# Loading the key weights before the first filter piece, and starting TensorE on the key blocks

## The chip, the cores and the metric

The kernel runs on one core of a Trainium2 chip. The core has five engines with instruction streams of their own: TensorE (PE: matrix products, with PEld for the loading of weights), VectorE (DVE), ScalarE (ACT), GpSimd (POOL) and SyncE (SP, which here only issues transfers). Sixteen DMA engines carry the transfers. The metric is the device time of one execution in microseconds (us), and a kernel is compared by the median of its runs.

## The reference

Two independent computations on 2048 rows of 576 columns stand side by side in the output.

```python
# A: a short causal filter of k times v, then a long causal convolution along the rows
k_shift = sum over t of k_pad[:, t:t+S, :] * shift_k[:, ks-1-t]      # ks = 4 taps
kv  = k_shift * v
y   = irfft(rfft(pad(kv)) * rfft(pad(ssm_k)))[:S] + kv * ssm_D
a   = q * y
# B: linear attention, 32 heads of 18 columns
q, k, v = split(x @ wqkv);  phi = lambda t: where(t > 0, t + 1, exp(t)) + 1e-6
kv  = phi(k)^T v per head;  z = sum of phi(k)
b   = (phi(q) kv / (phi(q) z + 1e-6)) @ wo
out = concatenate([a, b], axis=-1)
```

## The kernel before

The convolution of part A is done as a two-stage Fourier transform by matrix products with constant tables. The filter `ssm_k` (`hs`, in five pieces of 128 or 96 columns) is turned by TensorE (the helper `h_piece`, L479), written from PSUM to the tiles `hT`, and multiplied in the first stage (`s1`, L510) with the table `Gsb`, which is loaded in two halves. One `s1` block is four products into a pair of PSUM banks, and ACT or DVE writes it to `Ch` (L241 for ACT, L243 for DVE). An `s1` block reads one half of `Gsb`: blocks 384, 390, 392, 382 of the first channel group the first half, blocks 378, 380, 386, 388 the second. `s2` (L560), `inv` and `inv2` (L615, L640) follow, for the filter and then for the signal.

Part B projects `x`. The first quarter of the rows comes as two pairs of row blocks (`x_pairs`): each pair is loaded (`x_sb`), its last 64 columns are copied to `x4` (L241 or L245), and TensorE turns it with the identity in `idw` (L366), eight products and two more for `x4`; the result goes to `xT` (L243 or L241). Then `kproj` (L688) makes ten products for a key block of 128 rows, ACT the exponential (L693) and DVE the rest of phi (L696). `qproj` (L710) does the same for queries, five products at a time. The other quarters of `x` are turned by transposing transfers (L388, L390).

Before data has come, TensorE works on constants: the op `fill` (L930) multiplies a tile of ones nine times, and each of `NF` ops `fil2` (L937) four times. Nothing reads the results.

The order of all work is written out by hand. `PLAN` is a list of ops, each with a letter for its engine (P TensorE, A ScalarE, D VectorE, G GpSimd, S SyncE) and the number in which it was recorded; an engine runs its ops in the order of the list. `PLACES` gives each buffer its address or PSUM bank in the same order of recording. The numbers that matter here: 844 is `fill`, 845 and 846 are `fil2`; S26 and S28 load the two pairs of `x`, S15 the identity, S54 and S53 the key weights `wk`; S369, S421, S363, S470, S476 load the filter pieces in that order, S19 and S18 the halves of `Gsb`, S56 and S55 the query weights `wq`. P30 and P32 turn the first pair of `x`, P36 and P34 the second. P92 and P89 are the first two key blocks, P95 the third. P373 and P370 turn the first filter piece, P422 and P424 the second, P366 and P364 the third, P471 the first half of the fourth.

All loads go through one queue of SyncE in list order, and SyncE has eight semaphores for them: a load waits until the load eight places before it in the list has landed. SyncE's order in the section on the change shows these waits as DMAHW and a number.

Of the kernel before, what the change touches and what calls it, by code (L numbers as in the profile page):

```python
# [29 lines left out]
EP, WX = True, False  # L30
PW, QE, NF = False, True, 2
ACC = [(0, 1), (2, 1)]
# [164 lines left out]
def kernel(  # L197
# [26 lines left out]
    P = Prog()  # L224
# [104 lines left out]
    if WX:  # L329
        load("wjb", Wr, lambda e: dma(e, Wr.t[:].rearrange("p d j -> p (d j)"), ap(A_shift_k, 0, [[0, 128], [1, 4 * D]])), 589824, 4608)  # L330
        for i in range(3):
            P.op("AD", lambda e, i=i: copy(e, Wj.t[:, :, CC * i:CC * i + CC], Wr.t[:, CC * i:CC * i + CC, :].rearrange("p d j -> p j d")),
                 rd=[Wr], wr=[(Wj, i)], name="wjx", n=4 * CC)
    else:
# [4 lines left out]
             rd=[wtok], wr=[(Wj, i) for i in range(3)])  # L339
# [414 lines left out]
    for t in range(5):  # L754
# [8 lines left out]
         wr=[(wo5, "m")])  # L763
# [7 lines left out]
    def kvmm(e):  # L771
# [8 lines left out]
        rd=[kps, cst], wr=[(kvb, 0)], name="kvev", n=504)  # L780
    P.op("D", lambda e: nc.vector.tensor_tensor(
        out=kvb.t[0:72, 4, 0:72], in0=kps.t[0:72, 1, 0:72], in1=maskbd()[0:72, 0:72], op=ALU.mult),
        rd=[kps, cst], wr=[(kvb, 1)], name="kvev", n=72)
    zps = psb(1, "zps")

    def zmm(e):
# [10 lines left out]
        rd=[zps, cst], wr=[(zsel, 1)], name="zev", n=32)  # L797
# [9 lines left out]
    for f in range(2):  # L807
# [21 lines left out]
        if PW:  # L829
# [7 lines left out]
            wr=[den], name="den+", n=256)  # L837
# [90 lines left out]
    def fmm(e):  # L928
        for j in range(9):
            nc.tensor.matmul(fps.t[:, 0, :], lhsT=cft.t[:, 0:128], rhs=cft.t[:], start=True, stop=True)  # L930
    P.op("P", fmm, rd=[cft], wr=[fps], name="fill", mm=[(512, 128, 128)] * 9)
    for i in range(NF):
# [29 lines left out]
PLAN = """  # L962
G7 D843 P844 P845 S26 S15 P30 G4 G6 A27 P846 P32 G2 G11 G12 G3 S369 P373 D31 S54 S53 G0 A375 P370 A371 A372 D33 S20
G376 S22 P92 A93 P89 D94 S28 G13 G29 P36 P34 A37 D35 S421 P422 A374 A23 S19 G5 P424 D425 A90 S363 A423 D91 P95 A96 D97
P441 A442 P433 P366 D367 P364 D365 G368 G377 G8 A434 S470 P431 P471 A432 P392 A393 D472 P390 D391 G475 P384 A385 S18
P378 D379 S56 P380 A381 S55 G426 S476 P388 P386 A387 P382 A383 P427 P435 A436 D389 D428 P439 A440 D394 D412 P429 A430
P437 A438 P137 D403 A138 D139 P98 A99 D100 S24 P417 P395 P419 A420 A418 A396 D443 P473 D461 D474 P149 S58 A150 P399
A400 P413 P401 P404 S41 D151 D452 P397 A398 P146 A147 A405 P140 A141 D142 P408 A409 A402 D148 S59 P479 A480 A414 S60
G42 G57 G1 G10 S25 D64 P143 P477 P459 A144 D145 G9 P464 A465 P462 A463 S40 A478 G481 P158 A159 D160 P161 P415 P466 D65
A460 P468 A469 A467 A416 A162 D163 P164 P152 S51 P406 P457 A458 A407 P410 A411 P444 A445 S50 G52 P191 P453 P455 D72  # L970
# [46 lines left out]
"""  # L1017
# [30 lines left out]
```

## Time and profile before

| | before |
|---|---|
| median of 3 runs | 155.97 us |
| the runs | 155.5, 155.97, 158.14 us |
| the profiled execution: device time | 156.14 us |
| its span, first to last instruction | 154.4 us |
| granted TensorE clock, mean | 0.997 |
| busy: PE / DVE / ACT / POOL | 147.8 / 136.2 / 134.6 / 63.9 us |

The profile is of one execution. The span leaves out 1.74 us of its device time, before the first and after the last instruction. The page divides the span in slices and names for each engine how busy it was; the chain of waits follows the work that ended last back to the start. Of SyncE's rows, the time shown is that of issuing a transfer and not of the transfer itself. When a transfer landed can be read where an engine waited for it.

### The profile page before, as it was taken

The page shows a single profiled execution, that of the slowest core. Times are in us where ns is not written, and L with a number is a line of the kernel's source. Part 1 is how long each engine was busy: PE and PEld are TensorE (multiplying, and loading weights), DVE is VectorE, ACT ScalarE, POOL GpSimd, SP SyncE. Part 2 cuts the span into 40 slices and gives each one's busy share as a digit, 9 for nine tenths or more (in the row PEclk, how much of TensorE's full clock was granted, in tenths as well). Part 3 has the DMA queues.
Part 4 walks back from the last instruction along what each step waited for, and adds up shares of the span by engine and source line. Part 5 has one row for each costly group of instructions (what it writes and reads, how often), then busy time and mean ns, then how long its engine had stood idle before and what let it go on. Part 6 is the DMA issues. An engine that isn't in the chain of part 4 may idle for free.

```text
span 154.4 us, 4061 instructions
## 1 busy us (share of the span) xinstructions
PE 147.8 (96%) x1609; PEld 115.9 (75%) x1609; DVE 136.2 (88%) x161; ACT 134.6 (87%) x247; POOL 63.9 (41%) x57
## 2 busy tenths in 40 slices
PE   6999999999999999999999999899999999999980
PEld 2489975664758789788888887668767899999970
DVE  1027999999999999899999999999899999999980
ACT  3068999999999979896999999999999999999760
POOL 6020406003164954611170669998590005307500
PEclk9999999999999999999999999999999999999998
DMA  5899998999891038007961797699998999955895
GB/s 138 273 397 289 278 217 363 202 178 243 318 400 42 0 67 358 0 0 132 287 252 57 231 218 211 201 280 288 387 388 327 373 377 302 204 151 143 253 310 155
DMA packets 26717, 35.84 MB, mean 232 GB/s; under 512 B 15882, under 2 KB 21003, under 8 KB 25930
## 3 DMA queue, kind: packets, MB, share of 16 engines
q1 hardware_dynamic: 25834, 32.96, 69.2%
q0 software_dynamic: 864, 2.62, 9.3%
q8 instruction: 12, 0.20, 0.5%
q14 instruction: 7, 0.06, 0.1%
HBM read 20.76 MB, written 4.99 MB: 167 GB/s over the span
## 4 chain that ended last, share of the span: by engine, by line
PE 91%; ACT 5%; DVE 1%; issue 0%
PE ps_all L710 15%; PE ps_all L899 13%; PE ps_all L739 13%; PE ps_all L688 13%; PE ps_all L615 9%; PE ps_all L510 9%; PE ps_all L640 5%; PE ps_all L560 5%; PE ps_all L479 3%; PE ps_all L930 3%; ACT Ch L241 2%; PE ps_all L937 1%; ACT sph L241 1%; DVE spu L243 1%; PE ps_all L821 1%; PE ps_all L366 1%
## 5 line engine op out<-in xcount | busy, mean ns | idle before, releaser
L710 PE MATMUL ps_all<-xT,wq 128*126 128x512 bf16 (+1 forms) x100 | 24.2, 382 | 0.0
L899 PE MATMUL ps_all<-M,pqT 126*128 126x288 bf16 (+1 forms) x160 | 22.5, 287 | 0.0
L688 PE MATMUL ps_all<-wk,xT 128*128 128x288 bf16 x160 | 20.9, 286 | 0.0
L445 DVE TENSOR_TENSOR m<-kh,Wj 128x6144 bf16<-128x6144 bf16 x6 | 20.1, 3348 | 0.0
L688 PEld LDWEIGHTS <-xT 128*128 128x128 bf16 x160 | 17.4, 110 | 2.9
L899 PEld LDWEIGHTS <-pqT 126*128 126x128 bf16 (+1 forms) x160 | 16.6, 110 | 3.2 <-issue 1.4
L710 PEld LDWEIGHTS <-wq 128*126 128x126 bf16 (+1 forms) x100 | 12.4, 132 | 7.7 <-issue 1.5
L260 POOL TENSOR_TENSOR m<-m 128x1536 bf16<-128x1536 bf16 x4 | 12.4, 3095 | 13.7 <-DVE pqT L257 6.3
L241 ACT ACTIVATE Cu<-ps_all 128x768 bf16<-128x768 f32 x22 | 17.6, 859 | 0.2 <-PE ps_all L510 0.2
L510 PEld LDWEIGHTS <-Gsb 128*128 128x128 bf16 x192 | 16.2, 98 | 2.0 <-issue 1.0
L739 PE MATMUL ps_all<-pk,x_sb 128*128 128x289 bf16 (+1 forms) x128 | 17.1, 287 | 0.0
L241 ACT ACTIVATE Ch<-ps_all 128x768 bf16<-128x768 f32 x20 | 15.7, 846 | 1.4 <-PE ps_all L510 1.4
L260 POOL TENSOR_TENSOR pqT<-pqT,rb 126x1024 bf16<-126x1024 bf16 (+1 forms) x7 | 15.3, 2195 | 3.6 <-DMA X<-sph 2.4
L241 ACT ACTIVATE sph<-ps_all 128x512 bf16<-128x512 f32 x31 | 16.6, 618 | 0.0
L241 ACT ACTIVATE V<-ps_all 128x512 bf16<-128x512 f32 x30 | 16.3, 645 | 0.1
L615 PE MATMUL ps_all<-Esb,sph 128*128 128x128 bf16 x144 | 15.7, 219 | 0.0
L696 DVE SCALAR_TENSOR_TENSOR pk<-ek,ps_all 128x576 bf16<-128x576 bf16 x16 | 11.8, 751 | 3.9 <-ACT ek L693 3.8
L241 ACT ACTIVATE spu<-ps_all 128x512 bf16<-128x512 f32 x27 | 14.6, 616 | 0.2 <-PE ps_all L560 0.2
L739 PEld LDWEIGHTS <-x_sb 128*128 128x128 bf16 x128 | 12.4, 98 | 2.9
L713 ACT ACTIVATE eq<-ps_all,neg 126x512 bf16<-126x512 f32 (+1 forms) x20 | 13.4, 705 | 1.0 <-PE ps_all L710 1.0
L615 PE MATMUL ps_all<-Esb,X 128*128 128x128 bf16 x112 | 13.7, 219 | 0.0
L615 PEld LDWEIGHTS <-sph 128*128 128x128 bf16 x144 | 12.9, 98 | 0.5 <-issue 0.4
(95 smaller groups left out, 304.1 us busy)
## 6 DMA issues: line engine op xcount, KB each, us to landing
X<-sph SPq DMA_DIRECT2D x18, 256.0 KB
v<-in_A_v_dram SPq DMA_DIRECT2D x2, 1152.0 KB
out_dram<-ob SPq DMA_DIRECT2D x16, 144.0 KB
q<-in_A_q_dram SPq DMA_DIRECT2D x1, 2304.0 KB
out_dram<-q SPq DMA_DIRECT2D x11, 192.0 KB
rb<-r_scr SPq DMA_DIRECT2D x8, 252.0 KB
x_sb<-in_B_x_dram SPq DMA_DIRECT2D x3, 576.0 KB
kh<-in_A_k_dram SPq DMA_DIRECT2D x1, 1584.0 KB
```

Of the source, the lines that this page charges most:

```text
L241: nc.scalar.activation(out=o, in_=i, func=ACTF.Copy)
L260: return (nc.vector if e == "DVE" else nc.gpsimd).tensor_tensor(out=o, in0=a, in1=b, op=op)
L445: return nc.vector.tensor_tensor(out=m.t[:], in0=i0, in1=i1, op=ALU.mult)
L510: nc.tensor.matmul(ps.t[:, bank, lo - 384 * bank:hi - 384 * bank], lhsT=Gsb.t[:, b, ri, :], rhs=src[:, lo - CC * j:hi - CC * j], start=Tru ...
L560: nc.tensor.matmul(ps.t[32 * j:32 * j + 32, kh - k0, :], lhsT=W2()[32 * kh:32 * kh + 32, :], rhs=ct.t[32 * kh:32 * kh + 32, 8 * j:8 * j + ...
L615: nc.tensor.matmul(ps.t[:, hh, 128 * c:128 * c + 128], lhsT=src.t[:, 4 * (h0 + hh) + c, :], rhs=Esb.t[:, 32 + wi, :], start=(wi < 2), stop ...
L688: nc.tensor.matmul(ps.t[:, hh, 0:HALF], lhsT=cols(xT.t[0:KT[t], t, :], r), rhs=wk.t[0:KT[t], t, HALF * hh:HALF * hh + HALF], start=(t == 0 ...
L696: P.op("D", lambda e: nc.vector.scalar_tensor_tensor(out=pk[r // 4].t[:, r % 4, 0:D].rearrange("p (h c) -> p h c", h=2), in0=eb.t[:], scal ...
L710: nc.tensor.matmul(ps.t[0:hn, c - c0, :], lhsT=wq.t[0:KT[t], t, HCH[c][0]:HCH[c][0] + hn], rhs=xT.t[0:KT[t], t, :], start=(t == 0), stop=( ...
L713: P.op("A", lambda e: nc.scalar.activation(out=eb.t[0:hn], in_=ps.t[0:hn], func=ACTF.Exp, bias=neg1.t[0:hn, :]), rd=[ps, neg1], wr=[eb], n ...
L739: nc.tensor.matmul(ps.t[0:m, 0, 0:n], lhsT=x4[r // 4].t[:, r % 4, :] if t == 4 else x_sb[r // 4].t[:, r % 4, 128 * t:128 * t + 128], rhs=p ...
L899: nc.tensor.matmul(ps.t[:, hh - h, 0:HALF], lhsT=cols(pqT[r // 8].t[0:128 if c == 4 and not EP else hn, c, 512 * (r // 4 % 2):512 * (r // ...
```

## The change

Four edits, nearly all in the list of the order.

- `fill` has five products in place of nine, and there is one `fil2` in place of two. The one that is left stands behind both turns of the first pair of `x`.
- The loads of the key weights (S54, S53) stand ahead of the load of the first filter piece (S369), behind the identity.
- The first two key blocks (P92, P89, with their work on ACT and DVE) stand ahead of the turns of the first filter piece (P373, P370). One of the three writes of that piece to `hT`, op 372, goes from ACT to DVE.
- The `s1` blocks 378 and 382 change places, their writes to `Ch` with them: the write at the earlier place stays on DVE and the one at the later place on ACT.

```diff
-PW, QE, NF = False, True, 2
+PW, QE, NF = False, True, 1
...
     def fmm(e):
-        for j in range(9):
+        for j in range(5):
             nc.tensor.matmul(fps.t[:, 0, :], lhsT=cft.t[:, 0:128], rhs=cft.t[:], start=True, stop=True)
...
-G7 D843 P844 P845 S26 S15 P30 G4 G6 A27 P846 P32 G2 G11 G12 G3 S369 P373 D31 S54 S53 G0 A375 P370 A371 A372 D33 S20
+G7 D843 P844 S26 S15 S54 S53 P30 G4 G6 A27 P32 P845 G2 G11 G12 G3 D31 D33 G0 S369 S20 S22 S28 P92 A93 P89 D94 A90 D91
...
-P378 D379 S56 P380 A381 S55 G426 S476 P388 P386 A387 P382 A383 P427 P435 A436 D389 D428 P439 A440 D394 D412 P429 A430
+D383 S56 P380 A381 S55 G426 S476 P388 P386 A387 P378 A379 P427 P435 A436 D389 D428 P439 A440 D394 D412 P429 A430 P437
```

SyncE at the program's start, before, with the waits on earlier loads (`hs` are the filter pieces; DMAHW0 is the semaphore of the first and the ninth load, DMAHW1 that of the second and the tenth, and so on):

```order
L234 DMA x_sb_3_74<-in_B_x_dram 128x1152
L234 DMA idw_76<-tab_i 128x288
L234 DMA hs_104<-in_A_ssm_k_dram 128x2048
L234 DMA wk_97<-in_B_wqkv_dram 64x576
L234 DMA wk_97<-in_B_wqkv_dram 128x4x576
L234 DMA Drow_134<-in_A_ssm_D_dram 1x576
L234 DMA srow_137<-in_A_shift_k_dram 64x36
L234 DMA x_sb_3_74<-in_B_x_dram 128x1152
L234 DMA hs_178<-in_A_ssm_k_dram 128x2048 [waits DMAHW0_49]
L234 DMA Gsb_191<-tab_g 128x2048 [waits DMAHW1_49]
L234 DMA hs_205<-in_A_ssm_k_dram 128x2048 [waits DMAHW2_49]
L234 DMA hs_255<-in_A_ssm_k_dram 96x2048 [waits DMAHW3_49]
```

And now:

```order
L234 DMA x_sb_3_66<-in_B_x_dram 128x1152
L234 DMA idw_68<-tab_i 128x288
L234 DMA wk_70<-in_B_wqkv_dram 64x576
L234 DMA wk_70<-in_B_wqkv_dram 128x4x576
L234 DMA hs_103<-in_A_ssm_k_dram 128x2048
L234 DMA Drow_105<-in_A_ssm_D_dram 1x576
L234 DMA srow_107<-in_A_shift_k_dram 64x36
L234 DMA x_sb_3_66<-in_B_x_dram 128x1152
L234 DMA hs_173<-in_A_ssm_k_dram 128x2048 [waits DMAHW0_49]
L234 DMA Gsb_186<-tab_g 128x2048 [waits DMAHW1_49]
L234 DMA hs_198<-in_A_ssm_k_dram 128x2048 [waits DMAHW2_49]
L234 DMA hs_247<-in_A_ssm_k_dram 96x2048 [waits DMAHW3_49]
```

The two key-weight loads have passed the first filter piece. From the sixth place on, the order of the loads is the same.

ScalarE's first work on data, before (`x_6` is `x4`, `ek` the exponentials of key blocks, `Ch` the writes of `s1` blocks):

```order
L241 ACTIVATE x_6_88<-x_sb_3_74 128x2x64
L241 ACTIVATE hT_13_120<-ps_all 128x8x64
L241 ACTIVATE hT_14_130<-ps_all 128x8x64
L241 ACTIVATE hT_13_120<-ps_all 128x8x64
L693 ACTIVATE ek_149<-ps_all,neg_12_118 128x576
L241 ACTIVATE xT_11_114<-ps_all 128x256
L241 ACTIVATE hT_14_130<-ps_all 128x8x64
L241 ACTIVATE srt_189<-srow_137 64x36
L693 ACTIVATE ek_203<-ps_all,neg_12_118 128x576
L241 ACTIVATE hT_13_120<-ps_all 128x8x128
L693 ACTIVATE ek_219<-ps_all,neg_12_118 128x576
L241 ACTIVATE Ch_226<-ps_all 128x4x96x2 x3
```

And now:

```order
L241 ACTIVATE x_7_83<-x_sb_3_66 128x2x64
L693 ACTIVATE ek_120<-ps_all,neg_11_101 128x576
L693 ACTIVATE ek_133<-ps_all,neg_11_101 128x576
L241 ACTIVATE hT_17_152<-ps_all 128x8x64
L241 ACTIVATE hT_19_157<-ps_all 128x8x64
L241 ACTIVATE xT_10_98<-ps_all 128x256
L241 ACTIVATE hT_19_157<-ps_all 128x8x64
L241 ACTIVATE srt_184<-srow_107 64x36
L241 ACTIVATE hT_17_152<-ps_all 128x8x128
L693 ACTIVATE ek_211<-ps_all,neg_11_101 128x576
L241 ACTIVATE Ch_218<-ps_all 128x4x96x2 x3
```

The exponentials of the first two key blocks come first, and one write to `hT` is gone from ScalarE. From the first `Ch` on, its order is the same but for the two exchanged blocks, which read alike.

More of the change, by code (lines that the diff above doesn't have):

```diff
@@ L928, in fmm @@
     def fmm(e):
-        for j in range(9):
+        for j in range(5):
             nc.tensor.matmul(fps.t[:, 0, :], lhsT=cft.t[:, 0:128], rhs=cft.t[:], start=True, stop=True)
-    P.op("P", fmm, rd=[cft], wr=[fps], name="fill", mm=[(512, 128, 128)] * 9)
+    P.op("P", fmm, rd=[cft], wr=[fps], name="fill", mm=[(512, 128, 128)] * 5)
     for i in range(NF):
@@ L962 @@
 PLAN = """
[L963 to L969 removed]
+G7 D843 P844 S26 S15 S54 S53 P30 G4 G6 A27 P32 P845 G2 G11 G12 G3 D31 D33 G0 S369 S20 S22 S28 P92 A93 P89 D94 A90 D91
+P373 P370 A375 G13 G29 A371 D372 G376 P36 P34 A37 D35 S421 P422 A374 A23 S19 G5 P424 D425 S363 A423 P95 A96 D97 P441
+A442 P433 P366 D367 P364 D365 G368 G377 G8 A434 S470 P431 P471 A432 P392 A393 D472 P390 D391 G475 P384 A385 S18 P382
+D383 S56 P380 A381 S55 G426 S476 P388 P386 A387 P378 A379 P427 P435 A436 D389 D428 P439 A440 D394 D412 P429 A430 P437
+A438 P137 D403 A138 D139 P98 A99 D100 S24 P417 P395 P419 A420 A418 A396 D443 P473 D461 D474 P149 S58 A150 P399 A400
+P413 P401 P404 S41 D151 D452 P397 A398 P146 A147 A405 P140 A141 D142 P408 A409 A402 D148 S59 P479 A480 A414 S60 G42
+G57 G1 G10 S25 D64 P143 P477 P459 A144 D145 G9 P464 A465 P462 A463 S40 A478 G481 P158 A159 D160 P161 P415 P466 D65
 A460 P468 A469 A467 A416 A162 D163 P164 P152 S51 P406 P457 A458 A407 P410 A411 P444 A445 S50 G52 P191 P453 P455 D72
```

2 rows, old and new, of the table PLACES are left out of this document.

## The prediction

> **What bounds the kernel now.** I read the page first: who is busy, and what the chain of waits is made of.
>
> ```profile
> PE 147.8 (96%) x1609; PEld 115.9 (75%) x1609; DVE 136.2 (88%) x161; ACT 134.6 (87%) x247; POOL 63.9 (41%) x57
> PE 91%; ACT 5%; DVE 1%; issue 0%
> ```
>
> TensorE is the bound by a long way. The waits of TensorE say the same: in the whole span its idle time is the start and two small gaps.
>
> ```profile
> PE ps_all L930 <- DVE cft L926: 1.5, 1, 1.5
> PE ps_all L850 <- ACT M L241: 0.3, 1, 0.3
> PE ps_all L560 <- DVE spu L243: 0.2, 1, 0.2
> ```
>
> So taking work from TensorE's front should pay in full, unless that work is only filling time in which data is on its way. The timeline of TensorE (start, length, line, count) shows the opening; L930 and L937 are the constant products, L366 the turns of `x`, L479 those of the filter, L688 key blocks, L510 `s1` blocks.
>
> ```profile
> 1.45 4.02 PE L930 MATMUL ps_all<-cft 128*128 128x512 bf16 x9 [1.45 <-DVE cft L926]
> 5.27 1.65 PE L937 MATMUL ps_all<-cft 128*128 128x512 bf16 x4
> 6.75 0.61 PE L366 MATMUL ps_all<-idw,x_sb 128*128 128x128 bf16 x8
> 7.20 1.03 PE L937 MATMUL ps_all<-cft 128*128 128x512 bf16 x4
> 8.06 0.28 PE L366 MATMUL ps_all<-idw,x 128*128 128x128 bf16 x2
> 8.17 1.16 PE L479 MATMUL ps_all<-idw,hs 128*128 128x128 bf16 x16
> 9.17 2.61 PE L688 MATMUL ps_all<-wk,xT 128*128 128x288 bf16 x20
> 11.62 0.28 PE L366 MATMUL ps_all<-idw,x 128*128 128x128 bf16 x2
> ...
> 12.18 1.16 PE L479 MATMUL ps_all<-idw,hs 128*128 128x128 bf16 x16
> ...
> 15.12 1.16 PE L479 MATMUL ps_all<-idw,hs 128*128 128x128 bf16 x16
> 16.17 0.49 PE L510 MATMUL ps_all<-hT,Gsb 128*128 128x192 bf16 x4
> 16.50 0.65 PE L479 MATMUL ps_all<-idw,hs 96*128 96x96 bf16 x8
> 16.98 5.24 PE L510 MATMUL ps_all<-hT,Gsb 128*128 128x192 bf16 x52
> ```
>
> From start to start, a constant product took (5.27 - 1.45)/9 = 0.424 us at first and (8.06 - 7.20)/4 = 0.215 us later: the clock doubles between 5.3 and 7.2 us, and the turns at 6.75 already run at (7.20 - 6.75)/8 = 0.056 us each.
>
> When the data lands is told by SyncE, which waits before issuing a load until the load eight places earlier has landed. Its timeline, its waits in the stretches 0 to 6.5, 6.4 to 8.7, 10.5 to 13 and 13 to 16.4 us, and ScalarE's first work on `x`:
>
> ```profile
> 6.45 1.11 SPq L234 DMA_DIRECT2D hs<-in_A_ssm_k_dram  x2
> 8.56 0.34 SPq L234 DMA_DIRECT2D Gsb<-tab_g  x1
> ...
> 10.08 0.51 SPq L234 DMA_DIRECT2D hs<-in_A_ssm_k_dram  x1
> 12.95 0.68 SPq L234 DMA_DIRECT2D w_scr<-srt  x1
> 16.31 0.33 SPq L234 DMA_DIRECT2D kh<-in_A_k_dram  x1
> ```
>
> ```profile
> SPq L234 <- DMA hs<-in_A_ssm_k_dram: 0.5, 1, 0.5
> SPq L234 <- DMA wk<-in_B_wqkv_dram: 1.0, 1, 1.0
> SPq L234 <- DMA hs<-in_A_ssm_k_dram: 0.4, 1, 0.4
> SPq L234 <- DMA hs<-in_A_ssm_k_dram: 1.0, 1, 1.0
> ```
>
> ```profile
> 3.64 0.31 ACT L241 ACTIVATE x<-x_sb 128x128 bf16<-128x128 bf16 x1 [1.63 <-DMA x_sb<-in_B_x_dram]
> ```
>
> Read together: the first pair of `x` landed by 3.64, the first filter piece by 6.45, the key weights by 8.56, the second filter piece at 10.08 + 0.51 + 0.4 = 11.0, the third at 12.95 + 0.68 + 1.0 = 14.6. TensorE turned that third piece at 15.12: 0.5 us behind its landing. The rest follows from the rate (busy times of stretches; the last column is GB/s, so thousands of bytes per us):
>
> ```profile
> 11.00:12.20 1.20, 1.20 (x18) 1.06 (x16) 0.76 (x1) 0.67 (x2) 0.14 (x1) 1.00 1.00 406
> 12.30:14.60 2.30, 2.30 (x30) 2.05 (x29) 1.91 (x3) 2.16 (x5) 0.00 (x0) 1.00 1.08 253
> 14.60:16.10 1.50, 1.50 (x24) 1.46 (x22) 0.85 (x3) 1.49 (x3) 0.00 (x0) 1.00 0.99 270
> 16.10:17.80 1.70, 1.70 (x25) 1.69 (x24) 1.70 (x4) 1.70 (x4) 0.38 (x1) 1.00 1.09 307
> ```
>
> The queue is full (DMA share, the column before, about 1.0) and serves loads in their order. The fourth piece, 96 x 2048 x 2 = 393 KB, needs 393/270 = 1.5 us after 14.6 and lands near 16.1; it is used at 16.50. The second half of `Gsb`, 524 KB, needs 524/307 = 1.7 us and lands near 17.8; block 378, the fourth from 16.98 at 0.33 us each, uses it near 18.0. These two are estimates. So behind a TensorE that never idles stands a transfer queue only 0.2 to 0.5 us ahead of it.
>
> **The change part by part.** *The shorter opening, by work alone.* Five products end at 1.45 + 5 x 0.424 = 3.57. The turns need the identity, queued behind `x`: 74 KB at 253 to 406 KB per us, 0.2 to 0.3 us after 3.64, say 3.9. The ten turns now run at the slow clock, 0.424/4 = 0.106 us each: 4.97. Four slow products: 6.67. The two key blocks take 11.62 - 9.17 = 2.45, to 9.12; the filter's turns 9.17 - 8.17 = 1.0, to 10.12. Before, this place is 11.62. By work alone the change is worth 1.50 us: 2.34 of constant products removed (3.82 + 1.48 + 0.86 before, 9 x 0.424 now), less 0.5 for turns at the slow clock and 0.33 of waiting.
>
> *The loads exchanged.* The key weights (664 KB) no longer wait behind 524 KB of filter. Between 6.45 and 8.56 the queue moved those 664 KB, 314 KB per us, so they land about 524/314 = 1.7 us earlier, at 6.9: 0.2 us after TensorE is ready for them, which moves 10.12 to 10.35. The first filter piece lands in their stead, by 8.56, ahead of its use at 9.35. On SyncE's queue the exchange passes nothing else; Drow, `srow` and the second pair of `x` stand behind the same sum of bytes as before. The key blocks also wait for the write of the turned `x`:
>
> ```profile
> 7.40 0.69 DVE L243 COPY xT<-ps_all 128x1024 bf16<-128x1024 bf16 x1 [6.00 <-PE ps_all L366]
> 8.37 0.29 DVE L243 COPY xT<-ps_all 128x256 bf16<-128x256 bf16 x1 [0.28 <-PE ps_all L366]
> ```
>
> Those are 0.98 us from about 4.9, done by 5.9 under the `fil2` products; without that cover they would hold the key blocks until 5.9, still ahead of the weights.
>
> *From 10.35 on, data decides.* The second pair of `x` was used at 11.62; SyncE's load at 10.08 waits for it and shows no wait, so it has landed by then. Its turns take 12.18 - 11.62 = 0.56, to 10.9. The second filter piece lands at 11.0: about 0.1 of waiting. From there to the third piece is 15.12 - 12.18 = 2.94 of work, to 14.0; the third piece lands at 14.6, so TensorE stands for 0.6 and starts at about 14.7, 0.4 ahead of now. To the fourth piece are 16.50 - 15.12 = 1.38, to 16.1, which is when it lands. I put its start at 16.2, a gain of 0.3; the ends are 0.1 (it is used now within 0.4 of its estimated landing) and 0.4.
>
> *The exchanged `s1` pair.* Block 382 needs only the first half of `Gsb`. With 378 in its place, TensorE would ask for the second half at 16.7 + 3 x 0.33 = 17.7 and wait 0.1 for 17.8; block 380, now the first to need it, comes at 18.0. The cover is worth at most 0.1. The other engine's side: the chain of waits goes over to ScalarE here.
>
> ```profile
> 17.15 0.35 PE ps_all L510 x4
> 17.49 0.02 issue
> 17.52 2.27 ACT Ch L241 x3
> ```
>
> ScalarE's write at 17.52 is released by TensorE's block at 17.15, so it moves with that block, by the same 0.3, and what follows with it. The writes exchanged between DVE and ScalarE are one for one, and op 372, moved to DVE, lies ahead of 14.6, where both wait for data: nothing.
>
> *Sum.* 1.50 by work, 1.2 of it lost to the queue: 0.3 gained, between 0 and 0.6. The profiled execution, 156.14 us (span 154.4 and 1.74 around it), becomes 155.85; it stands 0.17 above the median of the three runs. The median 155.97 becomes 155.7.
>
> **The rivals.** *The transfers come sooner* (25%). From 12.3 on the queue moves 253 to 307 KB per us, just before 406. No row names a reason, and it may not recur. At 406 the third piece lands at 12.3 + 524/406 = 13.6 and TensorE reaches it at 14.0 in place of 15.12: a gain of 1.1, to 154.9. Against it: the slow stretch holds over three different loads in a row.
>
> *The key weights land no sooner* (9%), if their rows of 1152 bytes are slow wherever they stand. At 8.56 the key blocks would end at 11.0 and the filter's turns at 12.05, 0.4 behind now; the third piece would be reached at 15.5, behind its landing, and 0.4 us stay: 156.4, slower. This decides from a landing later than about 8.1. For it: nothing else can run on TensorE in that wait, since the filter's turns now stand behind. Against it: the 314 KB per us above is no slower than the rows of the filter.
>
> *The clock comes later* (8%). [...]
>
> **How the numbers follow.** Forecast 58%, 155.7, its own range 155.2 to 156.1 (gain 0 to 0.6 and the spread of the runs, 155.5 to 156.1 without the one at 158.14). A range of 154.5 to 156.6 takes in the faster transfers and the milder slow cases. Two per cent, 3.1 us, is about what a measurement of this kernel can tell from no change; even the whole opening block, 6.2 us of which 2.3 go, is not enough for that: faster 2%. Slower by so much takes the late clock and more: 3%. Within: 95%.
>
> **What the changed kernel's profile would show.** TensorE starts the turns at 3.9 and the key blocks at 6.7 to 6.9. It now shows waits for `hs` at L479, about 0.6 us ahead of the third piece (near 14.0) and little ahead of the second and fourth; the constant work turned into idle time. The third piece starts near 14.7, the fourth near 16.2, ScalarE's `Ch` writes run on from 17.2, and after 22 us every row is as before, 0.3 us earlier. I am wrong if TensorE has no wait at the third piece (then the queue was sooner and the gain nears 1.1), if the key products start after 8 us, or if they take 0.245 us each beyond 10 us.

## The result and the profile after

The changed kernel took 158.57 us, median of four runs (158.21 to 159.26); the kernel before took 156.88 in the same comparison (four runs, 155.5 to 158.14). The ratio is 1.0147, with a 95% interval of 1.0107 to 1.0187: slower by about 1.5%, which is inside 2%, but outside the range of the prediction and on its other side. Three more measurements of the same kernel, told below, gave 1.0051, 1.0056 and 1.0061. The size of the loss differs, its sign does not. Ratios leave out executions more than 1.5% longer than the fastest of the same kernel and so need not equal the quotient of the medians, which are over all executions.

The profiled execution of the changed kernel took 159.26 us, its span 157.5. Its page, with the lines on the engines, on the granted clock over the span in 40 slices (9 is full) and on the chain of waits:

```profile
PE 149.2 (95%) x1601; PEld 116.4 (74%) x1601; DVE 137.2 (87%) x162; ACT 134.6 (85%) x246; POOL 64.0 (41%) x57
...
PEclk9999999999999999999999999956999999999998
...
PE 72%; DMA 13%; DVE 5%; ACT 4%; SPq 3%; issue 1%; DVEq 0%
```

The clock row before:

```profile
PEclk9999999999999999999999999999999999999998
```

TensorE issues eight matmuls less and is busy 1.4 us longer. The clock row shows why: near 102 us the granted clock falls. And the chain, which was 91% TensorE, now leads through transfers for 13% of the span. The opening itself came out as wished. TensorE's timeline:

```profile
3.78 1.01 PE L366 MATMUL ps_all<-idw,x_sb 128*128 128x128 bf16 x8
...
4.80 1.83 PE L937 MATMUL ps_all<-cft 128*128 128x512 bf16 x4
6.71 2.61 PE L688 MATMUL ps_all<-wk,xT 128*128 128x288 bf16 x20
...
11.58 1.17 PE L479 MATMUL ps_all<-idw,hs 128*128 128x128 bf16 x16 [0.71 <-DVE hT L243]
...
14.47 1.18 PE L479 MATMUL ps_all<-idw,hs 128*128 128x128 bf16 x16
...
15.88 0.65 PE L479 MATMUL ps_all<-idw,hs 96*128 96x96 bf16 x8
```

The third filter piece starts at 14.47 in place of 15.12, the fourth at 15.88 in place of 16.50. To see where that went, the start of the same matmul in both traces is enough. The table gives changed kernel minus kernel before, in us, at places named by the time before; two later profiles, of the kernel before and of the changed kernel, stand beside it.

| place (us before; line) | kernel before, again | changed | changed, third time |
|---|---|---|---|
| 12.18 L479 | -0.11 | -0.60 | -0.68 |
| 22.09 L710 | -0.08 | -0.54 | -0.62 |
| 81.60 L739 | +0.32 | -0.07 | -0.25 |
| 100.61 L560 | +0.63 | +1.08 | -0.25 |
| 105.37 L510 | +0.60 | +3.92 | -0.24 |
| 112.10 L899 | +2.11 | +3.92 | +0.48 |
| 114.60 L899 | +2.29 | +3.34 | +0.66 |
| span, us | 156.3 | 157.5 | 154.6 |

In the first profile of the changed kernel the gain of about half a microsecond lives until 78 us, shrinks at 80 and is lost at 99. The other two profiles in the table also lose 1.5 and 0.7 us between 105 and 112 us. The waits of TensorE in the changed kernel name the places:

```profile
PE ps_all L850 <- DMA wo<-in_B_wo_dram: 1.3, 1, 1.3
PE ps_all L479 <- DVE hT L243: 0.7, 1, 0.7
PE ps_all L510 <- DVE v L260: 0.3, 1, 0.3
```

At 80 us VectorE's products with the second half of the signal `v` come late, at 99 us the weights of the output projection, `wo`. TensorE's rows at L850, before and after:

```profile
99.73 0.94 PE L850 MATMUL ps_all<-wo,kvb 126*126 126x288 bf16 x6 [0.31 <-ACT M L241]
```

```profile
100.16 0.95 PE L850 MATMUL ps_all<-wo,kvb 126*126 126x288 bf16 x6 [1.25 <-DMA wo<-in_B_wo_dram]
```

The chain of waits goes over exactly these two transfers:

```profile
72.47 7.29 DMA v<-in_A_v_dram
...
79.85 0.96 DVE v L260
...
91.28 8.83 DMA wo<-in_B_wo_dram
...
100.16 0.47 PE ps_all L850 x2
```

Behind the second wait comes the clock. The stretches 98 to 102 and 102 to 104 us (busy times with counts; then granted clock, DMA share, GB/s):

```profile
98.00:102.00 4.00, 2.43 (x42) 1.38 (x30) 2.96 (x6) 2.97 (x6) 3.92 (x2) 1.00 0.47 160
102.00:104.00 2.00, 2.00 (x30) 1.02 (x20) 2.00 (x4) 1.91 (x5) 1.25 (x1) 0.50 0.94 304
```

TensorE is busy for 2.43 of 4 us, and then runs at half clock, by the trace's clock record from 101.98 for 6.83 us. That is the step from +1.08 to +3.92. In the same four microseconds the DMA engines were busy for 0.47 of the time (0.84 before), and between 96 and 98 us, with `wo` still on its way, for 0.28 of it (0.45 before). So the end of `wo` was not late for want of bandwidth.

So one execution tells a story: 0.5 us gained, 0.5 lost at `v`, 1.15 at `wo`, 2.8 at the clock, 0.6 made up again behind it. Of the four executions of the changed kernel only this one has the low granted clock (0.975 in the mean; 0.993 to 1.000 in the others), and the others still took 158.2 to 158.6 us. And the changed kernel's third profile, 154.6 us, has neither the wait for `wo` nor the clock's fall, and the kernel before has both 154.4 and 156.3. What belongs to the change and what to chance had to be found by runs.

### The profile page after: what moved, and what is told of

Read it like the earlier page. It is cut to its first block, busy times and chain, and to the rows that moved or that the text cites. A ratio compares the mean times of both kernels' runs of the same rounds, so it can differ in the third digit from the quotient of the medians.

```text
span 157.5 us, 4046 instructions
## 1 busy us (share of the span) xinstructions
PE 149.2 (95%) x1601; PEld 116.4 (74%) x1601; DVE 137.2 (87%) x162; ACT 134.6 (85%) x246; POOL 64.0 (41%) x57
## 4 chain that ended last, share of the span: by engine, by line
PE 72%; DMA 13%; DVE 5%; ACT 4%; SPq 3%; issue 1%; DVEq 0%
PE ps_all L710 14%; PE ps_all L899 14%; PE ps_all L688 13%; PE ps_all L615 9%; DMA wo<-in_B_wo_dram 6%; PE ps_all L640 5%; PE ps_all L560 5%; DMA v<-in_A_v_dram 5%; PE ps_all L510 4%; PE ps_all L739 4%; SPq L234 3%; PE ps_all L479 3%; DMA wk<-in_B_wqkv_dram 3%; DVE m L445 2%; ACT Ch L241 2%; DVE v L260 1%
## 5 line engine op out<-in xcount | busy, mean ns | idle before, releaser
L899 PE MATMUL ps_all<-M,pqT 126*128 126x288 bf16 (+1 forms) x160 | 24.4, 302 | 0.0
L710 PE MATMUL ps_all<-xT,wq 128*126 128x512 bf16 (+1 forms) x100 | 24.2, 382 | 0.0
L899 PEld LDWEIGHTS <-pqT 126*128 126x128 bf16 (+1 forms) x160 | 17.3, 114 | 4.4 <-issue 1.6
L510 PEld LDWEIGHTS <-Gsb 128*128 128x128 bf16 x192 | 16.6, 99 | 2.9 <-issue 1.7
L710 PEld LDWEIGHTS <-wq 128*126 128x126 bf16 (+1 forms) x100 | 12.4, 131 | 7.7 <-issue 1.5
L693 ACT ACTIVATE ek<-ps_all,neg 128x576 bf16<-128x576 f32 x16 | 11.5, 739 | 6.9 <-PE ps_all L688 6.1
L739 PE MATMUL ps_all<-pk,x_sb 128*128 128x289 bf16 (+1 forms) x128 | 17.1, 287 | 0.0
L241 ACT ACTIVATE spu<-ps_all 128x512 bf16<-128x512 f32 x27 | 14.6, 614 | 0.1
L739 PEld LDWEIGHTS <-x_sb 128*128 128x128 bf16 x128 | 12.4, 98 | 2.9
```

Of the source, the lines that this page charges most:

```text
L241: nc.scalar.activation(out=o, in_=i, func=ACTF.Copy)
L510: nc.tensor.matmul(ps.t[:, bank, lo - 384 * bank:hi - 384 * bank], lhsT=Gsb.t[:, b, ri, :], rhs=src[:, lo - CC * j:hi - CC * j], start=Tru ...
L693: P.op("A", lambda e: nc.scalar.activation(out=eb.t[:], in_=ps.t[:, :, 0:HALF], func=ACTF.Exp, bias=neg1.t[:]), rd=[ps, neg1], wr=[eb], na ...
L710: nc.tensor.matmul(ps.t[0:hn, c - c0, :], lhsT=wq.t[0:KT[t], t, HCH[c][0]:HCH[c][0] + hn], rhs=xT.t[0:KT[t], t, :], start=(t == 0), stop=( ...
L739: nc.tensor.matmul(ps.t[0:m, 0, 0:n], lhsT=x4[r // 4].t[:, r % 4, :] if t == 4 else x_sb[r // 4].t[:, r % 4, 128 * t:128 * t + 128], rhs=p ...
L899: nc.tensor.matmul(ps.t[:, hh - h, 0:HALF], lhsT=cols(pqT[r // 8].t[0:128 if c == 4 and not EP else hn, c, 512 * (r // 4 % 2):512 * (r // ...
```

## The experiments

### First: is it the late weights, chance, or the order?

Both kernels again, the changed kernel with `wo` loaded earlier, and the changed order with the old constants, on one chip.

**The changed kernel and the kernel before, unedited.**

> The changed kernel once more, nothing edited. Three theories stand against each other. LATE WEIGHTS: the opening's gain of about 0.55 us arrives at the end of the key stage, but TensorE then stands about 1.2 us at L850 for the output projection's weights (wo), and now and then the clock drops behind that wait; it expects that wait in this trace too, 1 us or more, and 157.5 to 159. CHANCE: wo lands early or late by luck in either kernel; it expects the wait to be gone about as often as not, and then 155.5. ORDER: something that the new order does on VectorE or the queues from 79 us on costs the 2 us whether or not TensorE waits at L850.

> The kernel before once more, nothing edited: how far two measurements of the same kernel differ, and whether its own slower executions (157.8 and 158.1 beside 155.5 and 156.0) show the wait at L850. LATE WEIGHTS expects a profile of 156 with no wait for wo above 0.3 us at L850; if the profile falls on 157.8, the wait should be there, 1 us or more. CHANCE expects the ratio to scatter by over 1% around 1.

The changed kernel: 157.86 (6 runs), ratio 1.0051, 1.0015 to 1.0087. The kernel before against itself: 156.98 beside 157.06, ratio 1.0015, 0.9976 to 1.0054. The changed kernel's profile has the wait for `wo` again (0.8 us). But so has the kernel before, in the profile of 156.3 us:

```profile
PE ps_all L560 <- DVE ob L243: 0.9, 1, 0.9
...
PE ps_all L850 <- DMA wo<-in_B_wo_dram: 0.4, 1, 0.4
```

So the execution on which the prediction rested was a favourable one. In all later comparisons the kernel before has medians of 156.85 to 157.09, not 155.97, and executions from 154.75 to 160.31 us.

**`wo` loaded earlier.**

```diff
-... G222 G85 P212 ... G264 S249 S250 P215 S226 A216 ... P514 S225 P281
+... G222 G85 S226 S225 P212 ... G264 S249 S250 P215 A216 ... P514 P281
```

> The changed kernel with the two loads of wo moved on SyncE's queue from behind the second pair of r_scr writes to right ahead of it. Nothing else moves. LATE WEIGHTS: wo lands before 98 us, the 1.3 us at L850 go, no clock drop follows, 155.3 (155 to 156), with the r_scr pair issued some 1 to 2 us later and the rb read behind it hidden. CHANCE: 155.3 as well, but then the kernel before must have been equally open to it. ORDER: 157 or more still. If the r_scr writes, now behind 0.65 MB, hold the rb reads of the next chunk that TensorE needs, another wait takes its place near 104 us and the time stays near 157.

159.19, ratio 1.0109 (1.0075 to 1.0143). The wait for `wo` is gone, as asked, but SyncE now waits up to 9.1 us for `r_scr` to land (5.7 in the changed kernel's first profile), and TensorE stands later, at L560, behind VectorE:

```profile
PE ps_all L560 <- DVE ob L243: 1.7, 1, 1.7
...
SPq L234 <- DMA r_scr<-rden: 11.2, 2, 9.1
```

The earlier load made another transfer later, as the expectation had allowed for. So this run does not show what the wait for `wo` alone is worth. That LATE WEIGHTS is not the whole of the cause is shown by a later profile of the unedited changed kernel, the fourth: it has no wait for `wo` and a span of 157.1 us.

**The changed order with the old constants** (17 products).

```diff
-PW, QE, NF = False, True, 1
+PW, QE, NF = False, True, 2
-        for j in range(5):
+        for j in range(9):
-... A27 P32 P845 G2 ...
+... A27 P32 P845 P846 G2 ...
```

> The changed kernel's order with the opening block back at its old length (nine products at the start and two blocks of four, 17 in place of 9). The opening then keeps its old start (turns near 5.3, key blocks near 8), the third filter piece is reached 0.1 to 0.3 us before it lands. If only TensorE being 0.55 us early at 72 us sets off the late stage (the loads issued in a new phase), this is 156.0, as before. ORDER: 158, as the changed kernel, since all its order is here. LATE WEIGHTS as a matter of bytes in the queue, whatever the phase: 157 to 158.5.

158.2, ratio 1.0069 (1.0052 to 1.0086), by the numbers the ORDER case. The trace says otherwise: here TensorE is 0.7 to 0.8 us behind the kernel before from 12 us on (the 0.71 us of waiting for VectorE is in it), so most of the 1.1 us is the opening's own. This run could not tell the theories apart.

### Second: the length of TensorE's code

The third part of the changed kernel's page has a queue for instructions (packets, MB, share):

```profile
q8 instruction: 12, 0.20, 0.5%
```

Twelve packets of 16 KB. Their times stand in the trace's packet records, and two of them, as the runs below show, move with the number of TensorE's matmuls. In the kernel before these two began at 54.3 and 72.3 us, in the changed kernel at 60.2 and 75.1. So in the changed kernel one falls into the transfer of `kh` (issued at 55.5) and one into that of `v` (72.5 to 79.8). The queues during these two transfers, first in the kernel before (56 to 63 and 73 to 79.5 us):

```profile
q1 hardware_dynamic: 144, 1.62, 66.5%
...
q1 hardware_dynamic: 563, 1.66, 68.5%
q0 software_dynamic: 130, 0.35, 31.9%
```

and in the changed kernel (55.5 to 63 and 72.5 to 79.8 us):

```profile
q1 hardware_dynamic: 144, 1.62, 63.3%
q8 instruction: 1, 0.02, 0.8%
...
q1 hardware_dynamic: 639, 1.74, 65.8%
q0 software_dynamic: 125, 0.33, 28.4%
q8 instruction: 1, 0.02, 0.8%
```

One fetch is 0.8% of sixteen engines over 7.3 us: 0.9 us of one DMA engine. By the packet records the two took 0.97 us (at 60.2) and 0.94 us (at 75.1). The change removes eight matmuls, each with its load of weights, ahead of everything else, so all later code stands earlier in TensorE's program. That gave a theory to test, CODE FETCH.

Eight matmuls less do not simply make a fetch later by eight matmuls. In all eleven profiles below with the old length of code or more, the fetch near 54 us begins within 0.4 us of TensorE's 461st product, and the load of `kh` is issued 1.6 to 2.6 us behind that product. In the nine with short code `kh` is issued 0.2 us behind it, and the fetch begins only 4.5 to 5.1 us behind it. That looks like a fetch which has come to stand behind the load in a queue; no run tested this reading. The next four expectations were written with CODE FETCH in mind.

**The kernel before with only the constants cut.**

```diff
-PW, QE, NF = False, True, 2
+PW, QE, NF = False, True, 1
-        for j in range(9):
+        for j in range(5):
-... P30 G4 G6 A27 P846 P32 ...
+... P30 G4 G6 A27 P32 ...
```

> The kernel before with only the opening block shortened (5 + 4 constant products in place of 9 + 4 + 4), every load and block in its old order. CODE FETCH (the new theory: the 8 matmuls less move every later fetch of TensorE's code, and in the changed kernel one falls at 75.0 to 75.5 us, inside the transfer of the second half of v, where the kernel before has it at 71.1 to 72.3, ahead of it): the fetch falls near 75 here too, v lands 7.2 us or more behind its issue, and 157.5 to 158.5 comes out although the order is the old one. ORDER: 156.5 to 157, the opening's gain (key weights still land near 8.5, third filter piece near 14.5, so at most 0.5) and no loss. QUEUE (from 80 us on transfers set the pace whatever TensorE does): 157.0, no change.

157.9, ratio 1.0076 (1.0031 to 1.0121): a loss without any of the new order. Fetches at 60.0 and 74.9.

**The changed kernel with eight tiny products**, which bring the code back to its old length:

```diff
             for j in range(4):
                 nc.tensor.matmul(fp2.t[:, 0, :], lhsT=cft.t[:, 0:128], rhs=cft.t[:], ...)
+            for j in range(8):
+                nc.tensor.matmul(fp2.t[:, 0, 0:32], lhsT=cft.t[:, 0:128], rhs=cft.t[:, 0:32], ...)
```

> The changed kernel with 8 small constant products of 32 columns put behind its second block, in the time that TensorE waits for the key weights: TensorE's code is as long as before the change, and the opening keeps its time (key blocks at 6.7 to 7.2). CODE FETCH: the fetch near 75.3 goes back to about 71.5, v lands in about 6.5 to 7 us, and the time falls to 156.5 or less. ORDER and QUEUE: 157.9, as the changed kernel, whatever the fetch does.

156.7, ratio 0.9978 (0.9949 to 1.0007); the median missed the 156.5 expected by 0.2. Fetches at 54.6 and 72.4. VectorE's timeline shows what that is worth when it works. In the kernel before and with the tiny products `v` has landed before it is asked for, and in the changed kernel it has not (a bracket names the idle time and who ended it):

```profile
79.68 0.96 DVE L260 TENSOR_TENSOR v<-m,v 128x1536 bf16<-128x1536 bf16 x1
```

```profile
79.78 0.96 DVE L260 TENSOR_TENSOR v<-m,v 128x1536 bf16<-128x1536 bf16 x1
```

```profile
79.85 0.96 DVE L260 TENSOR_TENSOR v<-m,v 128x1536 bf16<-128x1536 bf16 x1 [0.70 <-DMA v<-in_A_v_dram]
```

The first is the kernel before, its load of `v` issued at 73.00; the second the kernel with tiny products, issued at 73.10; the third the changed kernel, issued at 72.47. Issued 0.63 us earlier than with the tiny products, `v` was used 0.07 later. The tiny products do not always do this: in the second profile of the same kernel, told below, VectorE waits for `v` as long as in the changed kernel.

```profile
80.01 0.96 DVE L260 TENSOR_TENSOR v<-m,v 128x1536 bf16<-128x1536 bf16 x1 [0.68 <-DMA v<-in_A_v_dram]
```

**The wait that the change had put in, taken out.** The 0.71 us at 11.58 is the second filter piece's first half, op 422, waiting for its PSUM bank. ScalarE's and VectorE's rows (the first from ScalarE's timeline, then VectorE's) show the holder:

```profile
9.36 0.74 ACT L693 ACTIVATE ek<-ps_all,neg 128x576 bf16<-128x576 f32 x1 [0.42 <-PE ps_all L688]
9.99 1.07 ACT L241 ACTIVATE hT<-ps_all 128x512 bf16<-128x512 bf16 x2
```

```profile
11.10 0.42 DVE L243 COPY hT<-ps_all 128x512 bf16<-128x512 bf16 x1 [0.22 <-ACT hT L241]
```

With the key blocks in front, ScalarE has their exponentials to do first, then two writes of `hT`, and only then VectorE's write, op 372, frees the bank. The other half, op 424, has a free bank, so the two were exchanged:

```diff
-... S421 P422 A374 A23 S19 G5 P424 D425 ...
+... S421 P424 A374 A23 S19 G5 P422 D425 ...
```

> The changed kernel with the two halves of the second filter piece's turns exchanged on TensorE (op 424, whose PSUM bank is free, ahead of op 422, which waits 0.71 us for VectorE's write of op 372). Expected of all theories: the wait at 11.6 falls to about 0.2 and the third piece is reached 0.3 to 0.5 us sooner (13.9 to 14.2 on a run in which the key weights land at 6.7), unless that piece has not landed by then. On the end of the span: if the opening's time is carried through, 157.4 in place of 157.9. QUEUE: no change, 157.9 with 0.4 more of waiting at L850 or L560.

157.33, ratio 0.9997 (0.9955 to 1.004). The wait falls to 0.2 us. Between the turns of `x` at 11.62 and the third key block at 13.18, in the time of the kernel before, TensorE now loses 0.47 us of its lead; the unedited changed kernel lost 0.87 there. The third filter piece began at 14.62 and not at the 13.9 to 14.2 expected, since the key blocks began 0.3 us later than in the first profile of the changed kernel.

> Both edits together: 8 small products behind the second constant block, and op 424 ahead of op 422. CODE FETCH: 156.2 or less, the best of the set. QUEUE and ORDER: 157.4 to 157.9.

Both edits: 155.72, ratio 0.994 (0.990 to 0.998), the only one of these four below the kernel before by more than its interval. Its profile has a span of 153.5 us, fetches at 53.6 and 70.4, and these rows of TensorE:

```profile
10.54 0.67 PE L479 MATMUL ps_all<-idw,hs 128*128 128x128 bf16 x8
11.41 0.67 PE L479 MATMUL ps_all<-idw,hs 128*128 128x128 bf16 x8 [0.20 <-DVE hT L243]
...
13.91 1.17 PE L479 MATMUL ps_all<-idw,hs 128*128 128x128 bf16 x16
...
98.65 0.94 PE L850 MATMUL ps_all<-wo,kvb 126*126 126x288 bf16 x6 [0.31 <-ACT M L241]
```

The third piece at 13.91 and not 15.12, and at L850 no wait for `wo`.

### Third: controls, and a theory that fell

**The changed kernel a third time, and the tiny products at the very end**, where they move no fetch:

```diff
-... P305 D774 S775 A306 P303 A304 S307
+... P305 D774 S775 A306 P303 P846 A304 S307      (846: eight products of 32 columns)
```

> The changed kernel unedited, for the same chip as the three beside it: 157.5 to 158.5, code fetch near 75, the accumulating transfer (L450) issued after the fifth rb read, wait for wo at L850 of about 1 us.

> The changed kernel with 8 small products of 32 columns as the last work of TensorE, behind everything that matters, in place of behind the second constant block. Same number of products as in the kernel with the pad in front. CODE FETCH: only what stands ahead of 72 us shifts the fetch there, so it stays near 75 and the time stays at 157.5 to 158.5. If the pad in front helped in another way than by its place in the code (more products in all, a longer program), 156.7 here too.

157.98, ratio 1.0056 (1.0001 to 1.0111), and 157.53, 1.0035 (0.9995 to 1.0074). The first expectation failed in its details: this profile, the one of 154.6 us, has no wait for `wo`. The second kernel keeps the short code's fetches (60.5, 75.5) and stands between the two, nearer to the unpadded one; alone it decides nothing.

**The kernel before with the short constants, and the tiny products in front.**

> The kernel before with the shorter opening block and the 8 small products behind its second block: the old order, the old length of code. CODE FETCH: the fetch goes from 74.9 back to about 72, the 157.9 of the unpadded one falls to 156.5 or less (the opening's gain of 0.3 to 0.8 kept). Otherwise 157.9 again.

157.11, ratio 0.9978 (0.9936 to 1.002), where 1.0076 stood without them, on another chip. The median missed the 156.5 expected; the ratio fell by 1.0%.

**The fifth `rb` read moved.** In nine profiles the wait for `wo` went with the order in which the accumulating transfer (L450) and this read were issued.

```diff
-... S263 D70 S271 D71 ... G264 S249 S250 P215 ...
+... S263 D70 D71 ... G264 S249 S250 S271 P215 ...
```

> The changed kernel with the fifth rb read of the first group (72 rows, 147 KB, not used before 103 us) moved on SyncE's queue from ahead of the second r_scr pair to right behind it. So far, in nine profiles, the accumulating transfer issued 0.15 to 0.28 us AHEAD of that read goes with r_scr landing 8.5 to 8.7 us after its issue and no wait for wo, and issued 0.12 to 0.8 us BEHIND it with 9.5 to 10.2 us and waits of 0.4 to 1.3 us. If that order in the queue is what decides, then with the read out of the way r_scr lands within 8.7 us, the wait at L850 is 0.3 or less and the time 156.7 or less, although the fetch stays at 75 and v lands late. If the late v acts on another way (VectorE's work itself, or the same late transfer engine), 157.5 or more.

161.77, ratio 1.0265 (1.0174 to 1.0357). The wait for `wo` stayed at 1.3 us, and a new one came:

```profile
PE ps_all L510 <- POOL v L260: 2.6, 1, 2.6
```

That order was a mark of lateness, not its cause; the two profiles just told, the changed kernel's third and the one with the products at the end, break the pattern as well. The theory fell.

### Fourth: the place in the code, on one chip in five rounds

> The changed kernel unedited, beside the three below on one chip: 157.5 to 158.2, ratio to the kernel before 1.004 to 1.010; code fetch near 75.

> The changed kernel with the 8 small products behind the second constant block, once more and in more rounds: ratio 0.995 to 1.000 if the first measurement (0.9978, 0.9949 to 1.0007) stands, that is 0.7 to 1.0% below the unpadded kernel on the same chip; fetch near 72. If it comes out at 1.004 or more, the first was chance and CODE FETCH falls.

> The changed kernel with the 8 small products in the middle of the program (ahead of a query block near 54 us), where they cost TensorE about 0.1 to 0.3 us and leave the opening as it is. CODE FETCH: the fetch that falls at 75 goes to about 72, as with the pad in front, and the time comes down to 0.997 to 1.002 of the kernel before. If the pad in front helps through the opening itself (what TensorE or the queue does there), this one stays at 1.004 to 1.010, or higher by its own cost.

> The changed kernel with 16 small products behind the second constant block: code 8 products longer than before the change. CODE FETCH: the fetch goes to about 69, still ahead of v's transfer, so it is as good as with 8: 0.995 to 1.001. If it comes out at 1.004 or more, the place of that one fetch is not what decides, and something else in the length or the phase is.

The middle one puts the eight tiny products ahead of a query block near 54 us (`... A135 D136 G239 P846 P194 ...`; in the trace they ran at 49.5 us), the last has 16 in place of 8 in front. Measured:

| kernel | median, us | ratio | 95% interval | fetches |
|---|---|---|---|---|
| changed | 158.07 | 1.0061 | 1.0024 to 1.0099 | 60.8, 76.0 |
| 8 tiny in front | 156.40 | 0.9931 | 0.9893 to 0.9969 | 54.2, 71.8 |
| 8 tiny near 54 us | 157.27 | 1.0004 | 0.9961 to 1.0047 | 54.2, 70.7 |
| 16 tiny in front | 156.69 | 0.9972 | 0.9930 to 1.0014 | 52.7, 70.8 |

Three came out in the ranges that CODE FETCH had set, the second below its own (0.995 to 1.000). Eight products that nobody reads make the kernel 1.3% faster in front and 0.6% in the middle, where they take TensorE's time (in front, the eight took 0.42 us). In the middle version the opening is untouched, so a better opening is not what helps there, though the intervals of the first and third rows overlap a little. Nor is the opening better with the products in front: at 22 us these three profiles (8 products, twice, and 16) stand 0.73 us ahead to 0.11 behind the kernel before, the four of the changed kernel 0.62 ahead to 0.45 behind. What the front seems to gain over the middle is not explained.

### Last: two controls

> The changed kernel with the 8 small products in front and op 424 ahead of op 422, a second time and in more rounds: 0.990 to 0.996 of the kernel before, if the first measurement (0.994) stands; v used 6.7 to 7.2 us after its issue, code fetches near 54 and 71.

> The kernel before with 4 small products added in each of its two second-type constant blocks (8 in all), nothing else. CODE FETCH: the kernel before already has its fetch ahead of v, so moving it further ahead (to about 69 or 70) brings nothing, and the 0.2 to 0.4 us of the added products fall in time that the transfers fill: 0.998 to 1.003. If the small products help by themselves, whatever the code's length, 0.990 to 0.995 here too.

The version that had beaten the kernel before came out at 0.9991 (0.9949 to 1.0033) the second time: not confirmed as more than equal to the kernels with tiny products alone (the medians were 156.16 and 156.85 us). It missed both the ratio and the 6.7 to 7.2 us for `v`, which took 7.41. The kernel before with eight tiny products more: 1.0002 (0.9954 to 1.0049), so they help only where they restore the length.

### What all the profiles say together

The trace records when each of the sixteen engines finishes its part of a transfer. Per kernel (and profile): the two fetches, by how much the last part of `kh` came behind the fifteenth, the time from the issue of `v` to VectorE's first product with it, and the wait for `wo` at L850.

| kernel | fetches, us | `kh`: last part behind, us | `v`: issue to use, us | wait for `wo`, us |
|---|---|---|---|---|
| before, twice | 54.3, 72.3; 54.5, 71.1 | 0.01; 0.05 | 6.69; 7.25 | 0; 0.4 |
| before + 8 tiny | 53.3, 70.9 | 0.03 | 6.78 | 0 |
| before, short constants + 8 tiny | 54.9, 71.5 | 0.10 | 6.88 | 0.7 |
| changed, old constants | 55.2, 73.4 | 0.05 | 6.98 | 0.8 |
| changed + 8 tiny, twice | 54.6, 72.4; 54.2, 71.8 | 0.11; 0.18 | 6.69; 7.37 | 0; 0.2 |
| changed + 16 tiny | 52.7, 70.8 | 0.10 | 6.96 | 1.1 |
| changed + 8 tiny near 54 us | 54.2, 70.7 | 0.12 | 7.57 | 0.7 |
| changed + 8 tiny, 424 first, twice | 53.6, 70.4; 54.2, 72.2 | 0.05; 0.08 | 6.69; 7.41 | 0; 0.4 |
| **changed, four times** | 59.7 to 60.8, 74.9 to 76.0 | 0.95; 0.91; 0.66; 0.58 | 7.39; 7.34; 7.30; 7.32 | 1.3; 0.8; 0; 0 |
| **changed, `wo` early** | 60.1, 75.0 | 0.92 | 7.42 | (moved) |
| **before, short constants** | 60.0, 74.9 | 1.37 | 7.52 | 0.8 |
| **changed, 424 first** | 60.5, 75.4 | 1.22 | 7.64 | 0 (0.8 for ScalarE) |
| **changed, tiny at the end** | 60.5, 75.5 | 1.36 | 7.68 | 0 |
| **changed, fifth `rb` later** | 60.0, 75.1 | 0.83 | 7.28 | 1.3 |

The `kh` column separates the two groups without an exception: at most 0.18 us in eleven profiles with the fetch ahead of the transfer, 0.58 to 1.37 in nine with the fetch inside it. In the changed kernel's first profile the fetch took 0.97 us and the last part came 0.95 us behind, as if the fetch held one DMA engine for its own length. And the load is ready with its last part: in the same profile the fifteenth part of `v` landed at 79.08, the sixteenth at 79.76, and VectorE began with it at 79.85. `kh` has time to spare; `v` has none. Its column averages 7.02 us in the first group and 7.43 in the second (**bold**), and only the first has values below 7.28. That is 0.4 us of the loss. It is a difference of means: for `v` the last part comes late in every profile, 0.21 to 1.35 us behind the fifteenth in the first group (mean 0.83) and 0.68 to 1.86 in the second (mean 1.22), so something else makes a last part late there too, and the fetch only adds to it.

The rest is less settled. In the four profiles with `v` used within 6.8 us there is no wait for `wo`; of the other fifteen in which it was not moved, ten have one of 0.4 us or more. The clock fell near 101 to 102 us in five profiles, all with a wait for `wo` of 0.8 us or more. So a late `v` goes with a late `wo`, and the clock's fall with a long wait, which is a pattern and not a shown cause. But how lateness at 80 becomes lateness at 99, across a queue that runs empty near 82 us, no run showed. Nor do these profiles show the two groups apart in the wait for `wo` as the times show them apart. One slow profile has neither of the last two marks: the fourth of the changed kernel, 157.1 us, shows no wait for `wo` and no fall of the clock, but 1.4 us at 140.8 in which TensorE stood for nothing that the profile shows, with no fetch within 2 us.

The loss between short and restored code is shown by five comparisons, 0.6 to 1.3% or 0.9 to 2.0 us by the ratios and 0.5 to 1.1% by the medians (front, middle and 16 products above; the short constants, 1.0076 to 0.9978, on two chips; op 424 first, 0.9997 to 0.994, where the second measurement gave 0.9991). Old length alone is not enough: the changed order with the old constants stands at 1.0069, with an opening 0.7 to 0.8 us late. 0.4 us of the loss has a traced path; what makes up the rest is open.

## Why the prediction was wrong

**What held.** The turns were to start at 3.9 (3.78), the key blocks at 6.7 to 6.9 (6.71), the `Ch` writes to move with TensorE (17.52 became 16.90), and the exchanged `s1` pair to be worth nothing much: no wait shows there. The gain in the opening was to be 0.3 us with ends of 0 and 0.6; at 22 us the four profiles of the changed kernel have 0.54, 0.07 and 0.62 us of gain and 0.45 of loss. The late clock did not come: the clock was granted in full from 6.41 us in the first profile (6.51 before), and from 5.33, 4.84 and 4.79 in the others. None of the four shows a doubling later than before, so what one would cost was not shown.

**What held by two errors.** The sum lost 1.2 us to the queue, 0.6 of them in front of the third filter piece, which was to land at 14.6. SyncE saw it landed at 13.63, and in the other three profiles at 14.47, 12.63 and 14.30 (14.03 in the kernel before, the second time); TensorE waits for it in none of them. So the landing taken from one execution was the mis-sized term, and the rival that the transfers come sooner was right so far. The gain did not go to 1.1, since 0.71 us were lost at 11.58 to something the prediction had costed at nothing. Its sentence on op 372, "ahead of 14.6, where both wait for data: nothing", looked at the engine that took the write and not at the bank that the write frees. With op 424 first, 0.4 of that comes back.

The key weights' landing also varies more than was allowed: the key blocks start at 6.71 in the first profile of the changed kernel, 7.18 in the second and 7.70 in the fourth. In the fourth TensorE is 0.39 us behind the kernel before at 12.18: in effect the rival of the late key weights, in one profile of four, though it had its limit at 8.1 us; the 0.7 us of waiting for the bank are in it.

**The step that failed.** The sentence is "after 22 us every row is as before, 0.3 us earlier." The order of every engine behind 22 us is indeed the same, and in the first profile the rows are 0.5 us earlier until 78 us. But the eight matmuls were booked only as 2.34 us of TensorE's time. They were also code, a cost put at nothing, and their removal moved a fetch from 72 to 75 us, into the one transfer that VectorE waits for. In its place the runs showed a loss of 0.6 to 1.3% from the missing code. Of that 0.4 us lie at `v`; how the rest comes about stays open. No rival had a loss from behind the opening.

**The base.** The forecast stood on one execution with `v` used in 6.69 us and no wait for `wo`. The kernel before reaches that in some executions only; its longer measurements have medians near 157. The spread of 155.5 to 158.14 in three runs was a hint, and the prediction set the highest aside when it gave its own range.

**Was the opening worth what was said?** With the code's length restored, the changed kernel measures 0.9978, 0.9931 and 0.9972. Their mean, 0.996, is 0.6 us of 157, but only one of the three intervals leaves out 1, and the version with the products near 54 us measures 1.0004. The kernel before with the shorter constants and the tiny products, in the old order, measures 0.9978 as well. So some tenths of a microsecond of the shorter constants may reach the end once the side effect is taken out, and no run shows that the new order adds to them.

The cost of a fetch did not show at the engine that runs the code: TensorE has no wait at these two fetches, but the last part of `kh`, with a fetch inside its transfer, is late by 0.6 to 1.4 us.

## What to carry to other kernels

Removing instructions can move later fetches of that engine's code (here two, from 54.3 and 72.3 to 60.2 and 75.1 us); in a kernel whose transfers land just in time, look where the fetches fall before and after, and compare at equal code length before blaming or praising an order. A forecast of a few tenths of a microsecond needs more than one profile of the kernel before: find out first which of its waits come and go between executions. And where a write moves to another engine, ask whose PSUM bank it frees (TensorE stood 0.71 us for one here).

## What the runs showed of the hardware

- One fetch of instructions (16 KB) took 0.9 to 1.9 us on one DMA engine (0.88 to 1.29 in the first profile of either kernel) and, inside the load of `kh`, went with a last sixteenth that came 0.58 to 1.37 us behind in nine profiles of nine; without a fetch inside it was at most 0.18 us in eleven.
- The whole stretches in the clock's record were multiples of 3.413 us: in full for 95.57 us (28), halved for 6.83 (2) and in full again for 47.79 (14) in the changed kernel's first profile, in full for 146.77 (43) in that of the kernel before. In every one of the five profiles in which the clock fell near 101 us, it was granted in full for 95.57 us and then halved for 3.41 or 6.83 us. In the changed kernel's first profile TensorE was busy for 2.43 of the 4 us ahead of the fall, and not idle for longer than 1.25 us at a stretch. What makes it fall these runs do not show.
- The same program differs from one execution to the next by over 1%: the kernel before had profiled spans of 154.4 and 156.3 us, the changed kernel 154.6 to 157.5.
